# Sliding-window attention and a mixer layer on one core: the first channel weight loaded as full rows in two tiles, batch 1's scores in 64-row bursts without padding, and batch 0's output product by thirds of its weight

## The chip, the cores and the metric

The kernel runs on one core of a Trainium2 chip. The metric is the device time of one execution in microseconds (us). The engines are named as the profile names them: PE is the matrix engine (TensorE), DVE the vector engine, ACT the scalar engine, POOL the gpsimd engine and SP the queue that issues most transfers.

## What is computed

Eight batches, eight heads, 576 positions, 64 values per head. Heads 0 to 3 look back over 32 positions, heads 4 to 7 over 128 in steps of 4; a token-mixing and a channel-mixing layer with four weights follow. Inputs and output are float32.

```python
# attention, per batch b and head h (scale 1/8)
scores = scale * q @ k.T                      # 576 x 576, rel = row - column
mask   = (0 <= rel < 32) if h < 4 else (0 <= rel < 128 and rel % 4 == 0)
x[:, 64*h : 64*h+64] = softmax(where(mask, scores, -1e9)) @ v
# mixer, per batch
u   = x + (relu(x.T @ w_tok1) @ w_tok2).T     # w_tok1 576 x 256, w_tok2 256 x 576
out = u + relu(u @ w_ch1) @ w_ch2             # w_ch1 512 x 1536, w_ch2 1536 x 512
```

## The kernel before

**Stages.** The program is a prologue for batch 0 (its attention and token mixing) and then eight stages, `for b in range(B)` (line 1006). The main line of stage b is `gen_main(b)` (line 747): for each of 12 blocks `mb` of the hidden layer a product `gp` with the first channel weight (line 768), a relu into the tile `gt` (line 771), and then the output product `yp` of `gt` with the second channel weight `w4` (lines 787 and 807), to which `u` is added on the way out (line 797). Batches go in pairs: an odd batch also carries the 64 last positions of both (`gt` at line 759, `yp` at line 807). Beside the main line, stage b holds the attention values and token mixing of batch b+1 and the transposes and scores of batch b+2; stage 0 holds all of batch 1's attention as well, since the prologue covers batch 0 alone.

**Who sets the order.** All order is written by hand. `interleave` (line 816) walks through the main line, which yields the time that its author gave each piece, and drops each step of a list `(due time, cost, function)` in once that clock has passed the due time. Within an engine instructions run in the order in which they were emitted; between engines they wait on semaphores. So a due time sets a place in five queues at once (PE, DVE, ACT, POOL and SP), and every DMA that a step issues takes its place in SP's or POOL's queue.

**Scores.** Two forms exist. `scores_plain` and `scores_dil` (lines 453 and 479) serve batches 0 and 1: one matmul per head and block over 128 rows, in which the other head's 64 rows of queries are zero (the tile `qz`), and ahead of each a matmul with the identity that puts a large negative number (`veil`) where the mask forbids (line 423). `scores_twin` (line 498) serves batches 2 to 7 (`twinned`, line 345): the two heads of a pair stand on rows 0 to 63 and 64 to 127, a matmul for each in turn (line 510), with no padding and no veil; the mask is multiplied in after the exponential by POOL (`mask` and `mask_tails`, lines 552 and 567). A burst `g` covers two head pairs in six PSUM banks and 24 matmuls. `bare_steps` (line 363) makes the transposed queries and keys for batch 2's bursts on PE; from batch 3 on the transposes are DMAs (`dma_steps`), and POOL copies the keys into place (`place_steps`). `values` (line 592) multiplies with v; `mix_steps` (line 729) places token mixing (`h1p`, `up`) and the transposes `tpu` of `u`, whose copies `uT` feed the next stage's `gp`.

**PSUM.** There are eight banks: three with the tag `main`, three with `fl`, two with `sc`. A new tile in a bank waits until every reader of the last one there is done. A twin burst takes both `sc` banks, all three `fl` banks and one `main` bank.

**Weights.** `load_w3` (line 858) loads the first channel weight from POOL in three tiles of 512 of the 1536 columns, each as 512 pieces of 512 values, so that block `mb` needs tile `mb // 4` alone. The tiles are issued at lines 878, 881 and 984. The second channel weight `w4` comes in three thirds (line 988), four blocks `mb` each. `gate` (line 855) is a one-element copy on POOL that makes a batch's loads wait for something: batch 2's loads (lines 994 to 1001) wait for the first third of `w4`. POOL also casts nearly all inputs from float32 to float16 (`cast_steps`, line 274; `casts1`, line 981).

## Time and profile before

| | |
|---|---|
| time, median of 3 runs | 288.79 us (288.76 to 289.51) |
| the profiled execution's own time | 289.66 us |
| its span | 287.8 us |
| PE, busy | 276.8 us (96%) |
| POOL, ACT, DVE, busy | 163.0, 134.0, 132.1 us |
| chain that ended last | 80% PE, 8% DMA, 3% DVE, 3% POOL, 2% issue |
| granted clock of PE | 1.00 throughout (its upper level) |

The profile comes from one execution. Its span runs from the first instruction to the last; its own time also holds what lies around that. A matmul's record ends when its result is written, which is later than the moment at which the next can start: matmuls of 128x512 are recorded with 380 ns each and start 217 ns apart (0.65 us for three steps in the timeline of PE). So PE's pauses are read from starts and from the idle time in brackets, and not from its busy share. The first product of batch 0, `gp`, starts at 28.47 us, that of batch 1 at 69.24 us, and that of batch 2 at 105.06 us; these bound the two stages which the change touches. The page's line on DMA shows nine tenths or more in nearly every slice of 7.2 us up to 108 us, with one slice of three tenths (64.8 to 72 us).

### The profile page before, as it was taken

How to read it: one execution, taken by the hardware profiler on the slowest of the kernel's cores; microseconds unless marked ns; L12 is line 12 of the kernel's file. 1: busy time of each engine (PE TensorE's matmuls, PEld its weight loads, DVE VectorE, ACT ScalarE, POOL GpSimd, SP SyncE). 2: the span in 40 equal slices, each digit the busy share in tenths (PEclk: the TensorE clock that was granted, in tenths of full speed). 3: DMA queues.
4: the chain of work that ended last, by engine and by line, in shares of the span. 5: the costliest groups of instructions: out<-in, count | busy, mean ns of one | idle time of the engine just before them, and what ended most of it. 6: DMA issues, size and time to landing. Idle time of an engine off the chain costs nothing.

```text
span 287.8 us, 6995 instructions
## 1 busy us (share of the span) xinstructions
PE 276.8 (96%) x2838; PEld 210.9 (73%) x2838; DVE 132.1 (46%) x278; ACT 134.0 (47%) x265; POOL 163.0 (57%) x221
## 2 busy tenths in 40 slices
PE   5879999999999999999999999999999999999995
PEld 2777676888766886698776976797766966886594
DVE  7747658446764236414640164416440274421022
ACT  2854673263543804574447615482546534225500
POOL 6961860478865799449970999279952930000000
PEclk9999999999999999999999999999999999999999
DMA  7999999993999998979888978299974210431023
GB/s 218 263 211 218 283 225 207 320 218 82 328 210 192 264 264 230 139 164 350 226 159 182 330 224 186 57 219 329 193 150 95 85 64 2 91 112 37 0 76 108
DMA packets 105551, 52.63 MB, mean 183 GB/s; under 512 B 73872, under 2 KB 104464, under 8 KB 105520
## 3 DMA queue, kind: packets, MB, share of 16 engines
q1 hardware_dynamic: 101280, 47.07, 67.0%
q0 software_dynamic: 2640, 3.94, 8.0%
q10 hardware_dynamic: 1600, 1.18, 1.4%
q8 instruction: 22, 0.36, 0.6%
q14 instruction: 9, 0.07, 0.1%
HBM read 37.07 MB, written 9.44 MB: 162 GB/s over the span
## 4 chain that ended last, share of the span: by engine, by line
PE 80%; DMA 8%; DVE 3%; POOL 3%; issue 2%; ACT 2%; ACTq 1%; SPq 0%; POOLq 0%; DVEq 0%
PE yp L787 29%; PE gp L768 24%; DMA l_vd<-in_v_dram 4%; PE h1p L627 4%; PE yp L807 3%; DMA l_k<-in_k_dram 3%; PE up L639 3%; PE sc L510 3%; PE gt L759 3%; DVE xn L112 1%; DMA kr<-c_k 1%; PE h1p L625 1%; PE av L608 1%; PE up L650 1%; PE av L603 1%
## 5 line engine op out<-in xcount | busy, mean ns | idle before, releaser
L787 PE MATMUL yp<-w,gt 128*128 128x256 f16 x756 | 87.1, 273 | 0.0
L787 PEld LDWEIGHTS <-gt 128*128 128x128 f16 x768 | 78.6, 106 | 6.5
L106 ACT ACTIVATE gt<-gp 128x512 f16<-128x512 f32 x69 | 41.2, 597 | 76.3 <-PE gp L768 76.0
L768 PE MATMUL gp<-utd,w 128*128 128x512 f16 x144 | 54.7, 380 | 0.0
L768 PE MATMUL gp<-utm,w 128*128 128x512 f16 x144 | 54.6, 379 | 0.0
L768 PEld LDWEIGHTS <-w 128*128 128x128 f16 x384 | 39.2, 114 | 20.3 <-issue 0.5
L797 DVE TENSOR_TENSOR o<-yp,u 128x512 f32<-128x512 f32 x31 | 21.4, 691 | 63.1 <-PE yp L787 58.5
L112 POOL TENSOR_TENSOR attp<-attp,const 128x1280 f16<-128x1280 f16 x12 | 31.4, 2616 | 27.5 <-ACT attp L534 27.4
L112 DVE TENSOR_TENSOR xn<-av,rec 128x320 f16<-128x320 f32 x64 | 31.4, 491 | 2.2
L112 POOL TENSOR_TENSOR attd<-attd,const 128x1024 f16<-128x1024 f16 x12 | 25.3, 2132 | 1.6 <-ACT attd L534 1.6
L768 PE MATMUL gp<-uT,w 128*128 128x512 f16 x96 | 25.8, 379 | 0.0
L108 DVE TENSOR_SCALAR gt<-gp 128x512 f16<-128x512 f32 x27 | 18.5, 686 | 13.6 <-PE gp L768 13.1
L645 DVE TENSOR_TENSOR u<-up,xn 128x512 f16<-128x512 f32 x26 | 17.9, 690 | 7.5 <-PE up L639 7.5
L534 ACT ACTIVATE attp<-sc 128x480 f16<-128x480 f32 (+1 forms) x36 | 16.1, 536 | 7.4 <-PE sc L510 7.4
L102 POOL CAST c_k<-l_k 128x512 f16<-128x512 f32 x29 | 18.0, 628 | 1.9 <-DMA l_k<-in_k_dram 1.7
L102 POOL CAST c_q<-l_q 128x512 f16<-128x512 f32 x27 | 16.8, 629 | 3.1 <-DMA l_q<-in_q_dram 3.1
L616 DVE RECIPROCAL rec<-av 128x5 f32<-128x5 f32 x64 | 12.2, 190 | 13.8 <-PE av L613 13.7
L106 ACT ACTIVATE h<-h1p 128x256 f16<-128x256 f32 x29 | 11.1, 384 | 14.5 <-PE h1p L627 14.1
L399 POOL COPY kt<-kr 128x512 f16<-128x512 f16 x10 | 10.7, 1075 | 9.0 <-DMA kr<-c_k 9.0
L697 ACT COPY utd<-utm 128x512 f16<-128x512 f16 x12 | 12.8, 1135 | 4.1 <-DMA utm<-u 4.1
L102 POOL CAST vv<-l_vn 128x256 f16<-128x256 f32 x32 | 12.0, 420 | 4.3 <-DMA l_vn<-in_v_dram 4.1
L112 POOL TENSOR_TENSOR attt<-attt,const 128x512 f16<-128x512 f16 x12 | 14.0, 1165 | 0.0
(147 smaller groups left out, 459.9 us busy)
## 6 DMA issues: line engine op xcount, KB each, us to landing
out_dram<-o SPq DMA_DIRECT2D x72, 128.0 KB, 3.1
l_q<-in_q_dram SPq DMA_DIRECT2D x15, 512.0 KB, 7.2
l_k<-in_k_dram SPq DMA_DIRECT2D x14, 512.0 KB, 7.1
l_vn<-in_v_dram SPq DMA_DIRECT2D x32, 128.0 KB, 6.6
l_vd<-in_v_dram SPq DMA_DIRECT2D x16, 256.0 KB, 4.6
w<-in_moe_w_ch_dram POOLq DMA_DIRECT2D x6, 512.0 KB, 7.6
lt<-in_q_dram SPq DMA_DIRECT2D x8, 128.0 KB, 4.6
l_vt<-in_v_dram SPq DMA_DIRECT2D x8, 128.0 KB, 4.9
```

The source lines that it names most:

```text
L102: eng.tensor_copy(out=out, in_=in_)
L106: nc.scalar.activation(out=out, in_=in_, func=AF.Relu)
L108: eng.tensor_scalar_max(out=out, in0=in_, scalar1=0.0)
L112: eng.tensor_tensor(out=out, in0=x, in1=y, op=ALU.mult)
L534: nc.scalar.activation(out=out, in_=in_, func=AF.Exp, scale=0.125)
L616: nc.vector.reciprocal(out=rec[:, :, 0], in_=av[:, :, 64])
L627: nc.tensor.matmul(out=p, lhsT=w[:, s, j], rhs=x[:, s, c], start=False, stop=(s == 3))
L645: nc.vector.tensor_tensor(out=u16(b, s), in0=blocks4(p), in1=blocks4(xn[b][:, s]), op=ALU.add)
L697: nc.scalar.copy(out=natural(uTd[:, cb - 2]), in_=uTm[i][:, cb].rearrange("p r m -> p m r"))
L768: nc.tensor.matmul(out=p, lhsT=w3_block(cb, mb), rhs=uT[(b, cb)][0], start=(i == 0), stop=(i == 3))
L787: nc.tensor.matmul(out=p[:, c], lhsT=gta[:, mb, a0:m0 + 512:4] if half else gta[:, mb, a0:a0 + 128], rhs=w4[mb][:, c], start=(mb == 0), st ...
L797: nc.vector.tensor_tensor(out=blocks4(o32), in0=blocks4(p), in1=u16(b, s), op=ALU.add)
```

## The change

- `load_w3` loads 256 of the 512 rows at a time, each row of 1536 values whole, into two tiles. Every block `mb` now needs both. Both are issued in the prologue: the first behind the first of batch 0's two `vd` casts and no longer ahead of both, the second in its old place. The third load is gone.
- Batch 1 becomes twinned. Its transposes come from `bare_steps(1)`. In its first burst the mask is multiplied in by POOL after the exponential, pair by pair; in its second the six banks are first filled with the veil by 20 matmuls with the identity (128 columns each), over which the score matmuls add.
- Batch 0's output product runs for row groups 0 to 2 side by side in the three `main` banks, a third of `w4` at a time; row group 3 follows as before.
- The relu of batch 0's blocks 0 to 7, 9 and 11 is on DVE (before: the odd ones).
- Two query casts and the two `vd` casts of batch 1 move from POOL to ACT; `w4`'s loads stand after the same cast as before, with two casts fewer ahead of them. Batch 2's gate and loads move behind batch 1's first mask on POOL.
- Due times in stages 0 and 1 are new. Among them: batch 2's first burst stands between the last transposes of batch 1's `u` and the first product of stage 1, and batch 3's two bursts come later among the output products of stage 1.

```diff
-    w3 = [fixed(f"w3_{i}", [128, 4, 512]) for i in range(3)]
+    w3 = [fixed(f"w3_{i}", [128, 2, DCH]) for i in range(2)]
...
     def twinned(b):
-        return b >= 2
+        return b >= 1
...
-        if b == 2:
+        if b <= 2:
             tags = tags[2:4] + tags[0:2] + tags[4:6]
...
+        veils = b == 1 and g == 1
+
         def twin(hp, banks, c, keys, queries):
+            ends = c.stop == (512 if banks is not small else 256)
             for h in range(2):
                 rows = slice(64 * h, 64 * h + 64)
-                n = c.stop - c.start
-                nc.tensor.matmul(out=banks[h][:, c], lhsT=keys(rows), rhs=queries(rows), start=True, stop=True)
+                nc.tensor.matmul(out=banks[h][:, c], lhsT=keys(rows), rhs=queries(rows),
+                                 start=not veils, stop=ends or not veils)
+
+        if veils:
+            for p in ps:
+                for r in range(4 if p not in small else 2):
+                    nc.tensor.matmul(
+                        out=p[:, 128 * r:128 * r + 128], lhsT=ident,
+                        rhs=veil[:, BLK + 128:BLK + 256] if p in small else veil[:, 0:128],
+                        start=(r == 0), stop=False)
...
-                if h and (g or b == 2):
+                if h and b == 1 and hp == 0:
+                    mask(0)
+                    mask_tails(0)
+                elif h and (b == 2 or (g and b > 2)):
...
+        if b == 1 and g == 0:
+            mask(1)
+            mask_tails(1)
...
-            return w3[mb // 4][:, cb, mb % 4:512:4]
+            c0 = 512 * (mb // 4)
+            return w3[cb // 2][:, cb % 2, c0 + mb % 4:c0 + 512:4]
...
-            relu(nc.vector if (mb % 2 == 1 if b == 0 else mb % 4 != 3 if b == 1 else mb in (1, 5)) else nc.scalar, gta[:, mb, m0:m0 + 512], p)
+            relu(nc.vector if (mb < 8 or mb % 2 == 1 if b == 0 else mb % 4 != 3 if b == 1 else mb in (1, 5)) else nc.scalar, gta[:, mb, m0:m0 + 512], p)
...
+        if b == 0:
+            ps3 = [bank("main", 3, f"yp_{b}_{s}") for s in range(3)]
+            for i in range(3):
+                for s, p in enumerate(ps3):
+                    for half in range(2):
+                        c = slice(256 * half, 256 * half + 256)
+                        for mb in range(4 * i, 4 * i + 4):
+                            nc.tensor.matmul(
+                                out=p[:, c],
+                                lhsT=gta[:, mb, s:512:4] if half else gta[:, mb, 128 * s:128 * s + 128],
+                                rhs=w4[mb][:, c], start=(mb == 0 and not half), stop=(mb == NMB - 1 and bool(half)))
...
-        c = slice(512 * i, 512 * i + 512)
-        nc.gpsimd.dma_start(out=w3[i], in_=moe_w_ch1[:, c].rearrange("(x p) c -> p x c", p=128))
+        nc.gpsimd.dma_start(
+            out=w3[i], in_=moe_w_ch1[256 * i:256 * i + 256, :].rearrange("(x p) c -> p x c", p=128))
...
-    load_w3(0)
     cast_vd(0, 0, nc.gpsimd)
+    load_w3(0)
     cast_vd(0, 2, nc.gpsimd)
     load_w3(1)
...
-    load_w3(2)
-    for i in (2, 3, 4, 5, 7, 6, 8, 9, 10, 11):
+    for i in (0, 1, 2, 3, 4, 6, 8, 9, 10, 11):
         casts1[i]()
...
+            steps += [(t, 0.25, f) for t, f in zip((2.8, 3.4, 5.0, 5.4, 6.0, 9.6, 10.2, 10.8, 11.4), bare)]
+            steps += score_steps(1, 7.2, 5.6, lag=0.25)
+            steps += [(6.2 + 0.6 * i, 0.0, lambda i=i: cast_qk(1, "q", 2 + i, nc.scalar)) for i in range(2)]
+            steps += at(9.0, 0.0, [loads2])
+            steps += [(12.5 + 0.1 * i, 0.0, lambda i=i: cast_vd(1, 2 * i, nc.scalar)) for i in range(2)]
...
-            scores2 = score_steps(2, 29.6, 4.4, lag=0.25)
+            scores2 = score_steps(2, 34.2, 4.4, lag=0.25)
...
-            steps += score_steps(3, 21.0, 4.6, lag=0.1)
+            steps += score_steps(3, 25.4, 4.6, lag=0.1)
```

How instructions stand at three places. First POOL in the prologue; `w` with 4x512 or 2x1536 is the first channel weight, `vv` and `vt` the casts of batch 0's v, `lt` the gate ahead of batch 1's loads. Before:

```order
L860 DMA w_0_84<-in_moe_w_ch_dram 128x4x512
L102 CAST vv_69<-l_vd_123 128x4x2x64 x2
L860 DMA w_1_85<-in_moe_w_ch_dram 128x4x512
L102 CAST vt_71<-l_vx_124 128x4x64
L883 DMA w1t_80<-in_moe_w_tok_dram 64x256
L885 COPY w2p_82<-w_81 128x512
L885 COPY w2p_83<-w_81 128x512
L856 CAST lt_589<-w2p_83 1x1
L102 CAST c_t_609<-lt_589 128x512
L102 CAST c_q_611<-l_q_0_585 128x512
L860 DMA w_2_86<-in_moe_w_ch_dram 128x4x512
```

After:

```order
L102 CAST vv_69<-l_vd_122 128x4x2x64
L904 DMA w_0_84<-in_moe_w_ch_dram 128x2x1536
L102 CAST vv_69<-l_vd_122 128x4x2x64
L904 DMA w_1_85<-in_moe_w_ch_dram 128x2x1536
L102 CAST vt_71<-l_vx_123 128x4x64
L928 DMA w1t_80<-in_moe_w_tok_dram 64x256
L930 COPY w2p_82<-w_81 128x512
L930 COPY w2p_83<-w_81 128x512
L901 CAST lt_588<-w2p_83 1x1
L102 CAST c_t_608<-lt_588 128x512
```

The first load moved behind one `vd` cast, the second kept its place, and the third, which stood among batch 1's casts, is gone. Second, DVE at the end of stage 0: `o` is the output of batch 0, `kt` and `kr` are batch 2's keys, `uT` the transposed `u` of batch 1, `gt` the first relu of stage 1. Before:

```order
L102 COPY uT_0_1240<-tpu_0_1239 128x640
L102 COPY uT_3_1254<-tpu_3_1253 128x640
L797 TENSOR_TENSOR o_0_2_1215<-yp_2_1214,u_0_499 128x512
L102 COPY uT_1_1282<-tpu_1_1281 128x640
L387 COPY kr<-tp_k_2_1303 128x512
L388 COPY kt<-tp_k_2_1303 128x128
L387 COPY kr<-tp_k_3_1316 128x512
L388 COPY kt<-tp_k_3_1316 128x128
L797 TENSOR_TENSOR o_0_3_1296<-yp_3_1295,u_0_499 128x512
L108 TENSOR_SCALAR gt<-gp_0_1346 128x512
```

After:

```order
L842 TENSOR_TENSOR o_0_3_1102<-yp_3_1101,u_0_498 128x512
L385 COPY kt<-tp_k_0_1187 128x512
L102 COPY uT_0_1208<-tpu_0_1207 128x640
L385 COPY kt<-tp_k_1_1215 128x512
L102 COPY uT_3_1222<-tpu_3_1221 128x640
L102 COPY uT_1_1230<-tpu_1_1229 128x640
L108 TENSOR_SCALAR gt<-gp_0_1291 128x512
```

The last output, two key copies and all three `uT` copies now stand in one row, with the relu of stage 1 right behind. Third, PE in stage 1, where batch 3's first burst `sc_3_0` begins. Before, among the 64 last positions' output product `yp_1_4`:

```order
L807 LDWEIGHTS gt_93
L807 MATMUL yp_1_4_1703<-w4_87,gt_93 128x512
L510 LDWEIGHTS kt_65
L510 MATMUL sc_3_0_0_1716<-qt_66,kt_65 128x160
L510 LDWEIGHTS kt_65
L510 MATMUL sc_3_0_1_1717<-qt_66,kt_65 128x160
```

After, among the next output product `yp_1_0`:

```order
L832 LDWEIGHTS gt_92
L832 MATMUL yp_1_0_1691<-w4_86,gt_92 128x256
L512 LDWEIGHTS kt_65
L512 MATMUL sc_3_0_0_1718<-qt_66,kt_65 128x160
L512 LDWEIGHTS kt_65
L512 MATMUL sc_3_0_1_1719<-qt_66,kt_65 128x160
```

The burst moved behind all of `yp_1_4` and three quarters of `yp_1_0`; the second burst moved from ahead of `yp_1_1` into `yp_1_2`.

## Rows read from the trace of the kernel before

**Rows 1.** Windows, by stage: elapsed us, then each engine's busy us; granted clock, DMA share, GB/s

```profile
28.47:69.24 40.77, 40.11 (x462) 31.88 (x460) 24.67 (x54) 20.26 (x42) 24.43 (x42) 1.00 0.99 233
69.24:105.06 35.82, 35.22 (x376) 26.22 (x375) 17.59 (x35) 17.34 (x36) 26.81 (x27) 1.00 0.98 243
105.06:287.80 182.74, 179.00 (x1728) 135.70 (x1726) 70.88 (x146) 81.41 (x155) 94.45 (x114) 1.00 0.64 153
```

**Rows 2.** Timeline, PE: start, us, line, tiles, shape; spacing of batch 1's score matmuls

```profile
36.03 0.19 PE L425 MATMUL sm<-qz,kt 128*128 128x64 f16 x1
...
36.18 0.19 PE L423 MATMUL sm<-veil,const 128*128 128x64 f16 x1
...
39.12 0.22 PE L425 MATMUL sc<-qz,kt 128*128 128x128 f16 x1
...
39.29 0.22 PE L423 MATMUL sc<-veil,const 128*128 128x128 f16 x1
```

**Rows 3.** Line 423's matmuls, batches 0 and 1 together: counts by shape

```profile
L423 PE MATMUL sc<-veil,const x56: 216/219/233, 7.9 to 42.3; 128*128 128x128 f16 x32, 128*128 128x160 f16 x24
L423 PE MATMUL sm<-veil,const x40: 190/193/220, 11.7 to 43.1; 128*128 128x64 f16 x32, 128*128 128x128 f16 x8
```

**Rows 4.** Chain of waits, 60 to 72 us: batch 2's two score bursts; start, us

```profile
60.51 0.75 PE sc L510 x24
...
70.26 0.71 PE sc L510 x24
```

**Rows 5.** Timeline, PE: the pauses of both stages, idle time and releaser in brackets

```profile
40.65 0.19 PE L423 MATMUL sm<-veil,const 128*128 128x64 f16 x1 [0.20 <-ACT attd L488]
...
48.70 0.30 PE L608 MATMUL av<-vv,attd 128*128 128x65 f16 x4 [0.20 <-DVE xn L112]
...
82.35 0.28 PE L625 MATMUL h1p<-xn,w1t 128*128 128x256 f16 x1 [0.39 <-DVE xn L112]
...
91.53 0.44 PE L510 MATMUL sc<-qt,kt 64*128 64x160 f16 x8 [0.21 <-POOL kt L399]
```

**Rows 6.** Timeline, POOL and PE, and line 860's landing times: the first channel weight

```profile
19.65 0.74 POOL L860 DMA_DIRECT2D w<-in_moe_w_ch_dram  x1
...
28.47 0.99 PE L768 MATMUL gp<-uT,w 128*128 128x512 f16 x3
...
DMA to landing us min/median/max: 6.9/7.8/7.8
```

**Rows 7.** Timeline, DVE: copies out of PSUM at the end of batch 0's stage

```profile
59.89 0.69 DVE L385 COPY kt<-tp_k 128x512 f16<-128x512 f16 x1 [0.35 <-PE tp_k L378]
...
64.06 0.49 DVE L102 COPY uT<-tpu 128x640 f16<-128x640 f16 x1 [1.29 <-PE tpu L667]
64.99 0.82 DVE L102 COPY uT<-tpu 128x640 f16<-128x640 f16 x1 [0.44 <-PE tpu L675]
65.73 0.68 DVE L797 TENSOR_TENSOR o<-yp,u 128x512 f32<-128x512 f32 x1
```

**Rows 8.** Timeline, ACT: batch 2's exponentials and a copy among them

```profile
62.46 1.53 ACT L534 ACTIVATE attp<-sc 128x480 f16<-128x480 f32 x3
63.81 0.76 ACT L100 COPY uT<-tpu 128x640 f16<-128x640 f16 x1
```

**Rows 9.** Timeline, PE and POOL: batch 4's first burst, its last mask, its first masked use

```profile
122.38 0.64 PE L510 MATMUL sc<-qt,kt 64*128 64x160 f16 x14
...
136.68 1.16 POOL L112 TENSOR_TENSOR attt<-attt,const 128x512 f16<-128x512 f16 x1
...
138.32 0.28 PE L608 MATMUL av<-vv,attd 128*128 128x65 f16 x4
```

**Rows 10.** Timeline, POOL, and line 988's issues and landing times: the second channel weight

```profile
42.81 0.41 POOL L102 CAST vt<-l_vx 128x256 f16<-128x256 f32 x1
...
L988 POOL DMA_DIRECT2D w<-in_moe_w_ch_dram x3: 541/548/548, 39.2 to 40.3; - x3
...
DMA to landing us min/median/max: 5.5/7.4/10.6
```

More of the change, by code (lines that the diff above doesn't have):

```diff
@@ L990, with loads2 @@
             in_=moe_w_ch2[512 * i:512 * i + 512, :].rearrange("(p i) c -> p i c", i=4))
-    for cast in casts1[12:]:
-        cast()
-    new_qk(2)
-    gate(l32[(2, "t")][0:1, 0, 0:1], w4[0][0:1, 0:1])
-    for nm in ("q", "k"):
-        load_tail(2, nm, nc.sync)
-    for h0 in (0, 4):
-        for nm in ("q", "k"):
-            load_qk(2, nm, h0, h0 + 4, nc.sync)
-    load_v(2)
+    casts1[12]()
+    casts1[13]()
+    cast_vx(1, nc.gpsimd)
+    def loads2():
+        new_qk(2)
+        gate(l32[(2, "t")][0:1, 0, 0:1], w4[0][0:1, 0:1])
+        for nm in ("q", "k"):
+            load_tail(2, nm, nc.sync)
+        for h0 in (0, 4):
+            for nm in ("q", "k"):
+                load_qk(2, nm, h0, h0 + 4, nc.sync)
+        load_v(2)
     def at(t0, dt, fs):
```

55 lines of the change are left out of this document (34 added, 21 removed).

## The prediction

> **What bounds the kernel.** I read the windows first. From 28.47 to 105.06 us, the stages of batches 0 and 1, PE is busy for 40.11 of 40.77 and 35.22 of 35.82 us at a granted clock of 1.00 (its upper level, 2.4 GHz); the reader is to see that PE bounds both, with 0.66 + 0.60 = 1.26 us of recorded idle time, while no other engine is busy for more than 32 us of 40 [rows 1]. After 105.06 the order of the work is unchanged; whatever is won must be won before. Two quantities decide: PE's column time, and its pauses. Since a 512-column record lasts 0.38 us but the next one starts 0.217 us later, a pause hides up to 0.16 us more than its bracket shows.
>
> **What is removed.** Batch 1's padded scores. The spacing of their matmuls is 0.15 us for five steps of 64 columns (0.03 each) and 0.17 us for three of 128 (0.057), so about 0.07 for 160 [rows 2]. Line 423 has, for batches 0 and 1 together, 24 matmuls of 160 columns, 32 + 8 of 128 and 32 of 64 [rows 3]; batch 1 has half, and line 425 one score matmul for each: 24 x 0.07 + 40 x 0.057 + 32 x 0.03 = 4.9 us. In their place stand two twin bursts, of 0.75 and 0.71 us as batch 2's are [rows 4], and 20 veil matmuls of 128 columns, 20 x 0.057 = 1.14: 2.6 us. **Gain 2.3 us**, all on PE and so on the path. The transposes of batch 1's queries and keys are as many columns as before, and the thirds of `yp` are the same 72 matmuls in another order: no change.
>
> The pauses of the two stages go too, since what they wait for moves. The four largest are 0.20 (exponentials of batch 1), 0.20 and 0.39 (`xn` on DVE) and 0.21 us (`kt` on POOL) in brackets [rows 5]; with 0.16 hidden in each, and the remaining 0.26 of recorded idle time, I get 1.9 to 2.4. **Gain 2.2 us**, near the upper end, since the small ones hide time as well. This is the generous half of the sum: it takes all that was there, and what comes is listed by itself.
>
> **What is added: six places where PE may wait.**
> - *First weight.* Block 0 of batch 0 now needs both tiles, the second at its third matmul: 28.47 + 0.43 = 28.9 us. The old second tile was issued at 19.65 us and landed 6.9 us later, at 26.6, and the old third had not been issued [rows 6]. Half a megabyte more now travels by then. If the larger pieces cost nothing extra the tile lands near 27; with the 3.5 us more that a tile's worth takes (landing at 23.1 after 7.8, then at 26.6), near 30.1. So 0 to 1.2; I take 0.25, nearer the early end, as a row of 1536 values goes in fewer, longer pieces.
> - *Bursts of batch 1.* The first waits for DVE's copy of the last-but-one key transpose: 0 to 0.2, taken 0.2 (a copy lasts 0.69, the steps are placed 0.6 apart).
> - *Keys.* Two transposes of batch 1 share a bank, whose two copies together last about one `kt` copy of 0.69 us [rows 7]: 0 to 0.25, taken 0.25.
> - *The end of stage 0.* The order of DVE shows the last output, `kt`, `uT`, `kt`, `uT`, `uT` in one row: 0.68 + 0.69 + 0.49 + 0.69 + 0.82 + 0.49 = 3.9 us [rows 7]. PE meanwhile has only three transposes of batch 2, four of `u` and batch 2's first burst, 2.6 us by the spacings above, and uses the last `uT` at the third matmul of `gp`, 0.65 (with two spacings and the first one's own) later: 3.9 - 3.25 = 0.6 us at the least. But one bank of the burst is that of `tpu_3`, free only after the fifth copy, 3.4 us into the row, where PE arrives after 2.0: 1.4 us. And one `tpu` must wait for ACT's `uT` copy of 0.76 us, which has stood behind exponentials of 0.51 us each [rows 8]: 2.0 us. I take 1.4.
> - *Batch 2's last key transpose* waits for a copy of queries on ACT, behind all exponentials of that batch: 0 to 0.6 (one exponential of 0.51 [rows 8] and the rest of a second), taken 0.4.
> - *Batch 3's masks.* In batch 4, from the start of a first burst to the end of the last mask it took 136.68 + 1.16 - 122.38 = 15.5 us, and the use followed at 138.32, with 0.5 to spare [rows 9]. By the order of the change PE reaches the same use 14.1 to 14.7 us after the first burst (three and a quarter output products of 2.6, two bursts, four `gp` of 0.87, small ones). Pause 0 to 0.8, taken 0.4, as that is the middle and POOL is idle at its start.
>
> Together 0.25 + 0.2 + 0.25 + 1.4 + 0.4 + 0.4 = **2.9 us come**, between 0.6 and 5.05.
>
> A rule of the Trainium skill speaks to the fourth place: "TensorEngine Tiling (Array Packing)", section Performance Considerations, says that tiling raises TensorE's throughput but not the rate at which PSUM is emptied. This trace agrees: a burst of 24 takes PE 0.75 us [rows 4], three of its exponentials alone 1.53 [rows 8]. By that rule alone the fourth term would be its upper end and the saving 1.0 us.
>
> **What costs nothing, and its cover.** The third load leaves POOL, and no engine waits for that place. Four more relus on DVE (0.69 us or less each) fall on stretches of four `gp` matmuls (0.87 us); if DVE's `xn` steps fall behind them, PE's pauses of the old kind come back. POOL gets four masks for batch 1 (of about 1.2 us [rows 9], the wide ones more) and loses four casts; it was busy for 24.43 us of 40.77 [rows 1], idle for longest right after the gate of batch 2, which is where the masks fall. ACT takes over four casts and was busy for half the stage [rows 1]. Batch 1's loads land about 1 us later, as the longer weight tiles are ahead of them, and the transposes that need them are placed some 0.5 to 1 us behind that; if that is gone, the first weight's wait simply moves there. The second weight is issued about 1 us sooner, since two casts ahead of it went; its first use is after 44 us, when before it had landed at 44.7.
>
> **The sum.** -2.3 - 2.2 + 2.9 = -1.6 us. The profiled execution has a span of 287.8 us and a time of 289.66, which is 0.87 above the median of 288.79; its span becomes 286.2, its time 288.06, and the same saving on the median gives **287.2 us**. With the ends: -2.3 - 2.4 + 0.6 = -4.1 (284.7) and -2.3 - 1.9 + 5.05 = +0.85 (289.6).
>
> **The rivals.**
> 1. *The banks turn over in time* (chance 0.24). The copies on DVE start before the last output does, and the DMA lands early: only 1.0 us of pauses come, and -2.3 - 2.2 + 1.0 = -3.5 gives 285.3. For it: DVE is busy for 24.67 of 40.77 us [rows 1], so no queue is long. Against it: the six copies have one row in the order.
> 2. *The waits eat the gain* (0.20). The places come at their upper ends, 4.5 to 5: 288.7 to 289.3, no change that can be told. For it: DMA is at 0.98 to 0.99 in both stages [rows 1], so a late load is late by much. Against it: six ends at once.
> 3. *Batch 1's v comes too late: slower* (0.14). The `vd` casts now stand on ACT, ahead of the second burst's exponentials, due near 44.6 us; before they stood on POOL, and the last cast of v ran at 42.81 [rows 10]. The second weight is now issued 1 us sooner beside v's loads; its last third took 10.6 us to land where others flew beside it, its first 5.5 [rows 10]. If `vd` lands that same 5.1 us later, near 48, ACT stands still, `sc` banks stay full and PE waits 3.3 us: -1.6 + 3.3 = +1.7, 290.5. It decides only from a landing later than about 45. Against it: v's loads are issued ahead of the weight's. The skill's "DMA: Bandwidth & Descriptors", section Queues, rings and completion order, has each DMA engine go round between queues packet by packet; the 10.6 against 5.5 us agrees, and by that a load issued earlier can still be overtaken.
>
> **How the numbers follow.** A measurement can tell 0.3%, 0.87 us, from no change. My forecast has 0.42, with its own range 286.2 to 288.3, a sixth of which lies within 0.87 us of before. Faster by more: 0.24 + 0.36 = 0.60. Within: 0.06 + 0.17 = 0.23. Slower: 0.14 + 0.03 (the second rival's tail) = 0.17. The range from 284.7 to 289.7 takes in the bounds and leaves out the third rival and a little of the first.
>
> **What would show it right or wrong.** In the changed profile PE's bursts of batch 1 should last about 0.75 and 0.71 us with 1.1 of veil, and `gp` of batch 2 start near 103.5 instead of 105.06, with 182.7 us from there to the end. The pauses should stand before batch 2's first burst or `gp_1_0` (61 to 68 us, released by DVE), at batch 2's last key transpose (ACT), and at batch 3's first masked values near 102 us (POOL). A third matmul of `gp_0_0` released by DMA much after 28.9 would show the first term mis-sized. The forecast is wrong if new pauses exceed 4.5 us, if `vd` holds ACT at 45 us, or if batch 2's stage no longer starts and runs as before.

## The result, and the profile after

The changed kernel takes 289.71 us (median of 20 runs), the kernel before 288.77 in the same runs: the ratio is 1.0043, with a 95% interval from 1.0023 to 1.0063. It is slower by 0.94 us, where 287.2 was forecast and 289.7 was the end of the range. Its runs also spread more, from 288.4 to 292.2 us, against 287.7 to 289.6 before. Medians here and below are of all runs, while the ratios leave out four slow ones, two of them at a granted clock of 0.75 throughout (360.42 us in experiment 6 and 358.82 us in experiment 8, where it is the profiled one, so that no row of experiment 8's profile is used).

The profile after comes from an execution of 289.61 us, at the median. The page's part 1 first, then the windows by stage (elapsed us, busy us of each engine, granted clock, DMA share, GB/s), cut at the first products of batches 0 to 3:

```profile
PE 275.1 (96%) x2810; PEld 208.4 (72%) x2810; DVE 131.3 (46%) x276; ACT 134.3 (47%) x267; POOL 166.6 (58%) x220
```

```profile
26.71:67.54 40.83, 37.08 (x418) 28.35 (x415) 23.64 (x49) 16.39 (x34) 23.48 (x38) 1.00 0.98 248
67.54:104.14 36.60, 36.26 (x396) 27.19 (x391) 17.94 (x38) 21.47 (x46) 27.16 (x27) 1.00 0.89 200
104.14:133.58 29.44, 28.87 (x293) 22.01 (x292) 12.72 (x27) 15.11 (x30) 24.43 (x30) 1.00 1.01 238
133.58:287.83 154.25, 150.30 (x1438) 113.69 (x1436) 58.11 (x119) 66.29 (x125) 73.63 (x87) 0.99 0.59 143
```

These answer to [rows 1]. Stage 0 is as long as before (40.83 against 40.77 us), but PE is busy for 37.08 of it instead of 40.11. Its work did shrink; the time was waited away. About 0.9 of these 3.03 us was only moved: sixteen transposes of batch 2, which stood in stage 0, now stand in stage 1, and that stage is longer by them. Stage 2 is longer by one pause, the last of those below. The page's chain of waits has 75% PE and 13% DMA, where it had 80% and 8%.

The pauses stand in the timeline of PE after (idle time and releaser in brackets):

```profile
28.55 2.78 PE L787 MATMUL gp<-uT,w 128*128 128x512 f16 x12 [1.25 <-DMA w<-in_moe_w_ch_dram]
...
32.34 0.40 PE L378 MATMUL tp_q<-const,c_q 128*128 128x128 f16 x4 [0.34 <-POOL c_q L102]
...
45.34 1.92 PE L811 MATMUL yp<-w,gt 128*128 128x256 f16 x16 [0.57 <-DMA w<-in_moe_w_ch_dram]
...
64.46 0.38 PE L682 MATMUL tpu<-const,u 128*128 128x128 f16 x4 [0.56 <-ACT uT L100]
...
66.08 0.23 PE L512 MATMUL sc<-qt,kt 64*128 64x160 f16 x1 [0.16 <-DVE kt L385]
66.81 0.63 PE L512 MATMUL sc<-qt,kt 64*128 64x160 f16 x13 [0.50 <-DVE uT L102]
...
71.30 0.38 PE L378 MATMUL tp_k<-const,c_k 128*128 128x128 f16 x4 [0.31 <-ACT qt L383]
...
109.55 0.20 PE L629 MATMUL av<-vt,attt 128*128 128x65 f16 x1 [0.57 <-POOL attt L112]
```

The reader is to see three kinds: waits for DMA or for a cast of what it brought (28.55, 32.34, 45.34), waits for copies out of shared banks (64.46 to 71.30), and one for a mask (109.55). With the 0.16 us that each bracket hides they are those of the table further below.

### The profile page after: what moved, and what is told of

The parts are those of the page before. It is cut to its first block, busy times and chain, and to the rows that moved or that the text cites. A ratio compares the mean times of both kernels' runs of the same rounds, so it can differ in the third digit from the quotient of the medians.

```text
span 287.8 us, 6938 instructions
## 1 busy us (share of the span) xinstructions
PE 275.1 (96%) x2810; PEld 208.4 (72%) x2810; DVE 131.3 (46%) x276; ACT 134.3 (47%) x267; POOL 166.6 (58%) x220
## 4 chain that ended last, share of the span: by engine, by line
PE 75%; DMA 13%; POOL 3%; DVE 2%; ACT 2%; issue 2%; SPq 1%; ACTq 1%; POOLq 0%
PE gp L787 23%; PE yp L832 23%; DMA l_k<-in_k_dram 6%; PE h1p L645 5%; PE up L657 4%; PE gt L778 4%; PE yp L852 4%; PE yp L811 3%; PE sc L512 2%; DMA w<-in_moe_w_ch_dram 2%; DMA l_vx<-in_v_dram 2%; DMA utm<-u 2%; PE h1p L643 1%; PE av L626 1%; PE av L621 1%
## 5 line engine op out<-in xcount | busy, mean ns | idle before, releaser
L832 PE MATMUL yp<-w,gt 128*128 128x256 f16 x684 | 77.9, 273 | 0.0
L832 PEld LDWEIGHTS <-gt 128*128 128x128 f16 x696 | 71.4, 106 | 5.6
L106 ACT ACTIVATE gt<-gp 128x512 f16<-128x512 f32 x65 | 38.9, 598 | 65.4 <-PE gp L787 65.1
L112 POOL TENSOR_TENSOR attp<-attp,const 128x1280 f16<-128x1280 f16 x14 | 36.6, 2612 | 35.1 <-ACT attp L545 35.0
L842 DVE TENSOR_TENSOR o<-yp,u 128x512 f32<-128x512 f32 x28 | 19.4, 691 | 59.8 <-PE yp L832 55.3
L108 DVE TENSOR_SCALAR gt<-gp 128x512 f16<-128x512 f32 x31 | 21.2, 686 | 16.3 <-PE gp L787 15.6
L787 PE MATMUL gp<-uT,w 128*128 128x512 f16 x96 | 24.4, 380 | 1.2 <-DMA w<-in_moe_w_ch_dram 1.2
L545 ACT ACTIVATE attp<-sc 128x480 f16<-128x480 f32 (+1 forms) x42 | 18.7, 540 | 14.7 <-PE sc L512 14.7
L112 POOL TENSOR_TENSOR attt<-attt,const 128x512 f16<-128x512 f16 (+1 forms) x14 | 15.2, 1089 | 0.0
L545 ACT ACTIVATE attd<-sc 128x512 f16<-128x512 f32 x28 | 14.4, 612 | 0.0
```

The costliest lines, as they stand in the source:

```text
L106: nc.scalar.activation(out=out, in_=in_, func=AF.Relu)
L108: eng.tensor_scalar_max(out=out, in0=in_, scalar1=0.0)
L112: eng.tensor_tensor(out=out, in0=x, in1=y, op=ALU.mult)
L545: nc.scalar.activation(out=out, in_=in_, func=AF.Exp, scale=0.125)
L787: nc.tensor.matmul(out=p, lhsT=w3_block(cb, mb), rhs=uT[(b, cb)][0], start=(i == 0), stop=(i == 3))
L832: nc.tensor.matmul(out=p[:, c], lhsT=gta[:, mb, a0:m0 + 512:4] if half else gta[:, mb, a0:a0 + 128], rhs=w4[mb][:, c], start=(mb == 0), st ...
```

## Experiments

The first theory (A) was that the first weight as whole rows holds up stage 0; its rivals were the end of stage 0 (B) and the late masks of batch 3 (C).

**1. The first weight in columns again**, in the changed kernel:

```diff
-    w3 = [fixed(f"w3_{i}", [128, 2, DCH]) for i in range(2)]
+    w3 = [fixed(f"w3_{i}", [128, 4, 512]) for i in range(3)]
...
-            return w3[cb // 2][:, cb % 2, c0 + mb % 4:c0 + 512:4]
+            return w3[mb // 4][:, cb, mb % 4:512:4]
...
+        c = slice(512 * i, 512 * i + 512)
+        nc.gpsimd.dma_start(out=w3[i], in_=moe_w_ch1[:, c].rearrange("(x p) c -> p x c", p=128))
...
+    load_w3(2)
```

> The changed kernel with the first weight in three tiles of 512 columns again (third load among batch 1's casts); the order of the prologue stays as changed. If the whole-row tiles are what costs (A), the wait of 1.25 us at the third matmul of the first product goes, batch 1's loads land some 1 to 1.5 us sooner and the two waits of 0.5 and 0.3 us at batch 1's first transposes go with it: 1.5 to 2 us less than the changed kernel, about 288.0. If the loss sits at the end of stage 0 (B) or in the late masks (C), it stays within 0.5 us of the changed kernel, 289.2 to 290.2.

Measured: 289.43 us, ratio 1.0037 (1.0020 to 1.0055): no different from the change. The wait at the first product and those at the first transposes went, but PE then reached the ninth block before the third tile and waited 1.3 us there (1.14 in brackets):

```profile
38.00 0.41 PE L786 MATMUL gp<-uT,w 128*128 128x512 f16 x1 [1.14 <-DMA w<-in_moe_w_ch_dram]
```

So in this kernel it is not the form of the load: either form makes PE wait.

**2. The new order of the prologue in the kernel before:**

```diff
-    load_w3(0)
     cast_vd(0, 0, nc.gpsimd)
+    load_w3(0)
```

> The kernel before with one edit: the first weight tile is issued behind the first of batch 0's two vd casts instead of ahead of both. In the changed kernel's trace the first product of batch 0 starts at 26.7 instead of 28.5 us, and I put that down to this order (v's loads no longer share the DMA engines with the weight, vt is cast 1.7 us sooner). If that is right, the first product starts near 26.8 here too and, as the first weight in columns needs one tile alone, up to 1.5 us come through: 287.3 to 288.3. If the earlier start has another cause, or the DMA sets the pace of stage 0 anyway, 288.5 to 289.0.

Measured: 288.85 us, 1.0013 (0.9995 to 1.0031): no gain. The first product started at 26.6 us, but stage 0 then lasted 42.55 us; PE waited 0.98 us in brackets for the cast of batch 1's first queries:

```profile
31.08 0.29 PE L309 MATMUL tp_q<-const,c_q 128*128 128x128 f16 x2 [0.98 <-POOL c_q L102]
```

These queries landed at 30.27 us, no earlier than in the first profile of the kernel before (30.06). Nor was the start at 26.6 us a lead: the unedited kernel, profiled again (experiment 12), starts its first product at 26.89 us, and there the queries land at 28.46.

**3 and 4. The burst behind the product; the masks earlier:**

```diff
-            steps += scores2[:10]
...
+            steps += [(0.8 + 0.25 * i, c, f) for i, (_, c, f) in enumerate(scores2[:10])]
```

> The changed kernel with batch 2's first burst moved from ahead of the first product of stage 1 to behind its first two matmuls. B: the 1.0 us before and in the burst (0.32 and 0.68 us) go, and at most 0.3 comes back where the third matmul of the product waits for the last uT; about 0.7 us less, 289.0. A or C: no change within 0.3 us, 289.4 to 290.0, since then another wait takes the place (ACT's exponentials and the values of batch 2 behind them).

```diff
-            steps += score_steps(3, 25.4, 4.6, lag=0.1)
+            steps += score_steps(3, 23.4, 4.6, lag=0.1)
```

> The changed kernel with both bursts of batch 3 due 2.0 earlier in stage 1 (23.4 instead of 25.4). C: the pause of 0.73 us at 108.8 us (the values of head 4 of batch 3 wait for POOL's last mask) goes, 0.6 to 0.8 us less, about 289.0. Against C: the keys' copies or the output bank of the earlier place stop PE for as long, 289.4 to 290.0.

Measured: 293.62 us (1.0178, 1.0153 to 1.0203) and 290.77 (1.0059, 1.0031 to 1.0087). Both missed. With the burst later, PE waited for ACT at batch 2's last transposes, and in stage 2 it stood still for batch 4's keys (the timeline of PE of that kernel):

```profile
70.15 0.38 PE L378 MATMUL tp_q<-const,c_q 128*128 128x128 f16 x4 [0.83 <-ACT attt L545]
71.26 0.33 PE L378 MATMUL tp_k<-const,c_k 128*128 128x128 f16 x3 [0.73 <-ACT qt L383]
...
125.35 0.38 PE L512 MATMUL sc<-qt,kt 64*128 64x160 f16 x6 [1.64 <-POOL kt L399]
126.68 0.44 PE L512 MATMUL sc<-qt,kt 64*128 64x160 f16 x8 [0.94 <-POOL kt L399]
```

POOL copies those keys from a DMA that SP issued at 119.39 us instead of 115.22 and that landed at 124.10 instead of 118.49.

With the masks earlier, the pause at batch 3's values went and two came inside the burst itself, 0.30 and 0.41 us: an exchange. The second, as the timeline of PE has it:

```profile
92.88 0.23 PE L512 MATMUL sc<-qt,kt 64*128 64x128 f16 x2 [0.23 <-DVE u L663]
```

The profile has DVE's `u` end it; POOL's copies of these keys had been done since 90.74 us.

**5 and 6. Fewer bytes, the same matmuls.** This tells DMA from PE. In both kernels the second half of the first weight (rows 256 to 511) is left out and the first half used twice:

```diff
-            return w3[cb // 2][:, cb % 2, c0 + mb % 4:c0 + 512:4]
+            return w3[0][:, cb % 2, c0 + mb % 4:c0 + 512:4]
...
-    load_w3(1)
```

> The changed kernel without the second tile of the first weight: blocks 2 and 3 of the contraction use the first tile again (the second half of the first channel weight is left out). No matmul less, 0.75 MB less of DMA ahead of batch 1's loads. If stage 0 is paced by what the DMA engines bring (first weight, batch 1, second weight, one behind the other), the wait of 1.25 us at the first product and those of 0.5, 0.3 and 0.7 us behind it all shrink: 2 to 3 us less than the changed kernel, 286.7 to 287.7. If PE's own pauses at the end of stage 0 are what costs, the first wait alone goes and is partly found again later: 288.5 to 289.3.

```diff
-            return w3[mb // 4][:, cb, mb % 4:512:4]
+            return w3[mb // 4][:, cb % 2, mb % 4:512:4]
...
-in_=moe_w_ch1[:, c]
+in_=moe_w_ch1[0:256, c]
```

> The kernel before with the same bytes left out (each of its three tiles loaded for the first 256 rows only, blocks 2 and 3 use blocks 0 and 1; the second half of the first channel weight is left out). If DMA paces stage 0 in both kernels, this one gains too, but less, since its PE has 2.3 us more to do in that stage: 287.6 to 288.3, and the changed kernel without these bytes is the faster of the two by 0.5 to 1.5 us. If not, no change: 288.3 to 288.8.

Measured: the changed kernel without these bytes 287.29 us (0.9960 of before, 0.9945 to 0.9975), which is 2.4 less than with them; the kernel before without them 288.04 (0.9986, 0.9971 to 1.0001), hardly less. Stage 0 in the windows of the first, then of the second:

```profile
26.82:64.99 38.17, 36.70 (x418) 28.65 (x415) 23.60 (x49) 16.29 (x34) 23.63 (x38) 1.00 0.98 244
```

```profile
26.69:67.45 40.76, 40.11 (x461) 31.87 (x459) 24.66 (x54) 20.26 (x42) 25.13 (x41) 1.00 0.94 226
```

In the kernel before PE needs 40.8 us for the stage with these bytes or without. In the changed kernel PE could be done in 38.2 and DMA does not let it. One load shows it, the first of batch 1's queries, issued at 22.5 to 22.8 us (KB, us to landing): in the kernel before (experiment 12), in the changed kernel, and in the changed kernel without these bytes:

```profile
l_q<-in_q_dram SPq DMA_DIRECT2D x1, 512.0 KB, 5.6
```

```profile
l_q<-in_q_dram SPq DMA_DIRECT2D x1, 512.0 KB, 8.8
```

```profile
l_q<-in_q_dram SPq DMA_DIRECT2D x1, 512.0 KB, 5.9
```

This is the larger part of the miss: DMA stood close behind PE. Of the 2.4 us, 1.8 stand in the profiles, where stage 0 takes 39.99 us in the mean of the changed kernel's four (experiments 13 to 15 and the one above); these four executions average 289.20 us, 0.5 below the median.

**7. The burst ahead of the transposes of `u`**, as in the kernel before:

```diff
-            scores2 = score_steps(2, 34.2, 4.4, lag=0.25)
+            scores2 = score_steps(2, 29.6, 4.4, lag=0.25)
```

(and batch 2's five transposes at their old due times)

> The changed kernel with batch 2's first transposes and first burst back where they stood before (among the output products of batch 0, ahead of the transposes of u). If the row of DVE copies and the shared banks at the end of stage 0 cost (B), the pauses of 0.72, 0.32 and 0.68 us there go and little comes: 1.0 to 1.7 us less, 288.0 to 288.7. If batch 2's loads set the time of that burst (its last key tile lands at 58.7 us), PE waits for them instead and the time stays at 289.2 to 290.

Measured: 291.20 us, 1.0094 (1.0061 to 1.0127). PE did not wait for batch 2's loads, as the rival had it, but for the banks that the burst had filled: a `tpu` stood for 1.38 us in brackets until ACT had done the exponentials:

```profile
66.98 0.38 PE L691 MATMUL tpu<-const,u 128*128 128x128 f16 x4 [1.38 <-ACT attt L545]
```

**8 to 11. Three places edited, alone and together.** The second weight issued earlier, batch 2's transposes earlier, batch 3's keys cast on DVE and its steps earlier:

```diff
-    for i in (0, 1, 2, 3, 4, 6, 8, 9, 10, 11):
+    for i in (0, 1, 2, 3, 4):
         casts1[i]()
...
-    casts1[12]()
-    casts1[13]()
+    for i in (6, 8, 9, 10, 11, 12, 13):
+        casts1[i]()
...
-zip((28.0, 30.0, 30.5, 31.4, 32.2), bare)
+zip((25.5, 26.3, 27.2, 28.2, 29.2), bare)
...
-            casts = cast_steps(3)
+            casts = cast_steps(3, nc.vector)
...
```

> The changed kernel with the second weight's loads issued two key casts and four v casts earlier on POOL (behind batch 1's fourth query or key cast, before the wait for l_k's second half). In the changed kernel the DMA engines are only half busy near 36 and 40 us, POOL waits for that l_k until 36.2, and PE waits 0.73 us for the first third of the weight. If what is lost is this lull and not DMA work as such, the third lands before 44.4, the pause goes, and batch 2's loads behind the gate come earlier by as much: 0.5 to 0.9 us less, 288.8 to 289.2. If the weight only takes v's place on the engines, v comes late for the values of batch 1 and nothing is won: 289.5 to 290.

> The changed kernel with batch 2's first five transposes 2.5 to 3.2 us earlier, between the output products and the u products of stage 0; the burst stays. The two key copies of 0.68 us then no longer stand between the last output and the last uT copies on DVE. If that row makes the pauses at the end of stage 0 (0.72, 0.32 and 0.68 us), about 1 to 1.4 us go: 288.3 to 288.8. If DMA paces this place too (batch 2's keys are cast at 55.8 to 57.5 us), the transposes wait and it stays at 289.4 to 290.

> The changed kernel with batch 3's key casts moved from POOL (behind batch 2's masks) to DVE, its query casts, DMA transposes, key copies and both bursts 2 us earlier. The edit before moved the bursts alone and only exchanged the pause of 0.73 us at the masks for 0.72 us at POOL's key copies. If those copies were late because POOL did batch 2's masks first, both pauses go: 0.6 to 0.8 us less, 288.9 to 289.1. If not, or if DVE's relus and u come late in turn: 289.5 to 290.2.

> The three edits together (second weight's loads earlier, batch 2's transposes earlier, batch 3's keys on DVE and its bursts earlier). If the pauses are independent places on PE's path, the gains add up: 2.1 to 3.1 us less than the changed kernel, 286.6 to 287.6, below both kernels. If DMA paces the stages, what one place wins is waited for at the next: no better than 288.7.

Measured: 293.44 us (1.0157, 1.0130 to 1.0184), 290.72 (1.0066, 1.0044 to 1.0088), 293.50 (1.0161, 1.0119 to 1.0203) and 298.35 (1.0345, 1.0323 to 1.0367). None won.

The earlier second weight overtook batch 1's v. The lines on DMA (KB each, median us to landing) show v's loads issued from 34.7 to 37.7 us, first in the changed kernel, then with all three edits (where the weight is issued at 35.0 instead of 38.3):

```profile
l_vd<-in_v_dram SPq DMA_DIRECT2D x2, 256.0 KB, 3.6
l_vt<-in_v_dram SPq DMA_DIRECT2D x1, 128.0 KB, 4.2
l_vx<-in_v_dram SPq DMA_DIRECT2D x1, 128.0 KB, 4.3
```

```profile
l_vd<-in_v_dram SPq DMA_DIRECT2D x2, 256.0 KB, 11.9
...
l_vt<-in_v_dram SPq DMA_DIRECT2D x1, 128.0 KB, 12.5
l_vx<-in_v_dram SPq DMA_DIRECT2D x1, 128.0 KB, 11.5
```

And why, from the lines on queues (packets, MB, share of the engines' time) of the latter between 40 and 44 us; q0 carries POOL's loads, q1 those of SP:

```profile
q0 software_dynamic: 204, 0.77, 94.8%
q1 hardware_dynamic: 203, 0.05, 9.6%
```

The two queues move about as many packets, 204 and 203. But 187 of the weight's are 4096 bytes long (the other 17 have 4 bytes), and v's are 256 bytes: so v gets 0.05 of 0.82 MB. ACT and PE show what follows (timelines of both):

```profile
47.96 1.28 ACT L100 CAST vv<-l_vd 128x512 f16<-128x512 f32 x2 [5.18 <-DMA l_vd<-in_v_dram]
```

```profile
49.56 1.01 PE L811 MATMUL yp<-w,gt 128*128 128x256 f16 x4 [2.83 <-ACT attt L545]
```

This is the third rival's chain, link by link, and its price: 2.83 us and what the bracket hides, where 3.3 was worked out. The eighth edit alone came 3.3 us above the changed kernel by the ratios.

The tenth edit's wait was of its own making: the casts of batch 3's keys stand on DVE ahead of `xn` of batch 2, and PE stood still for 2.39 us in brackets (timelines of DVE, POOL and PE):

```profile
76.12 1.75 DVE L102 CAST c_t<-lt 128x512 f16<-128x512 f32 x1
...
79.61 1.65 DVE L102 CAST c_k<-l_k 128x512 f16<-128x512 f32 x1
...
81.80 1.49 DVE L102 CAST c_k<-l_k 128x512 f16<-128x512 f32 x3
```

```profile
75.47 2.12 POOL L112 TENSOR_TENSOR attd<-attd,const 128x1024 f16<-128x1024 f16 x1
...
78.85 2.12 POOL L112 TENSOR_TENSOR attd<-attd,const 128x1024 f16<-128x1024 f16 x1
```

```profile
81.94 0.28 PE L643 MATMUL h1p<-xn,w1t 128*128 128x256 f16 x1 [2.39 <-DVE xn L112]
```

The loads had landed by 75.57 us. Two of the casts lasted 1.75 and 1.65 us, the next three 0.42 to 0.62 us each; the two long ones ran while POOL multiplied wide masks. That this made them long was not tested. The edit also kept the two pauses of 0.30 and 0.41 us in batch 3's first burst, so these were not, as its expectation had it, waits for POOL's copies behind the key casts.

The ninth edit shortened the pauses at the end of stage 0 in its profile (0.29, 0.51 and 0.68 us instead of 0.72, 0.24, 0.32 and 0.68), but put pauses of 0.24, 0.38 and 0.18 us among the `u` products and transposes before them, at 57.6 to 60.5 us: 2.28 us in all instead of 1.97. So it won nothing there. Its median was 1.0 us above the changed kernel's; what makes the rest of that is left open.

**12 to 15. More profiles.** One execution is a thin basis, so both kernels were profiled again, unedited.

> The kernel before once more, unedited, for a second profile: the profiled execution shown with it took 289.66 us, 0.9 above its median, and is no fair partner for the changed kernel's. In a profile near the median the first product of batch 0 should start before 28.5 us or stage 0 should be shorter than 40.8 us, and the product of batch 3 start near 132.8 instead of 133.8 us.

> The changed kernel once more, unedited, for a second profile. Its runs spread from 288.4 to 292.2 us, those of the kernel before from 287.6 to 289.6. In the profile at hand v's last loads of batch 1 land at 39.0 to 41.4 us, 3 to 4 us before they are needed, and the second weight is issued at 38.3. If the long runs are those in which the second weight overtakes v (as in the edit that issued it earlier, where v landed at 48 to 50 us), a run near 291 or above shows v's last loads landing after 45 us and a wait at the values or the output product of stage 0; one near 289 shows them before 43. If the length comes from the first weight, the wait at the first product is longer instead.

> As the run before: the changed kernel unedited. Long (290.5 and above) with v's last loads after 45 us, or short with them before 43, if the second weight overtaking v makes the spread.

> As the two runs before: the changed kernel unedited. Long (290.5 and above) with v's last loads after 45 us, or short with them before 43, if the second weight overtaking v makes the spread.

Measured: 288.01 us for the kernel before, 288.81, 288.86 and 289.51 for the changed one. The starts of the first products (timelines of PE) give the length of each stage:

```
                       first product   stage 0   stage 1   stage 2   from there to the end
before                        28.47     40.77     35.82     28.70    154.06
before, again                 26.89     40.85     35.70     28.70    154.04
changed                       26.71     40.83     36.60     29.44    154.25
changed, again (r2)           27.38     39.34     36.60     29.44    154.26
changed, again (r3)           27.05     39.73     36.60     29.44    154.26
changed, again (r4)           27.38     40.06     36.60     29.43    154.26
```

So the late first product of the first profile (28.47) was that execution's own, and not what the change improved. Stages 1 and 2 repeat to 0.1 us; stage 0 of the changed kernel varies by 1.5 us, with the wait for the first weight (0.2 to 1.4 us) and the one for the second (0 to 0.7). No execution of 290.5 us or more was caught, so whether the long runs are those in which v is overtaken stays open.

**16 to 18. The pauses behind the weights taken off.** Batch 1's third `u` transpose copied by ACT, batch 2's last queries by DVE, batch 2's transposes earlier, batch 3's last mask on DVE:

```diff
-        eng = nc.scalar if cb == 2 else nc.vector
+        eng = nc.scalar if cb == 2 or (b == 1 and cb == 3) else nc.vector
...
+            if nm == "q" and b == 2 and hp >= 2:
+                nc.vector.tensor_copy(out=qta[:, hp], in_=grid)
...
-            mult(nc.gpsimd, t, t, tails_seen[g])
+            mult(nc.vector if b == 3 and g else nc.gpsimd, t, t, tails_seen[g])
```

> The changed kernel with batch 2's first transposes earlier (as in the edit tried alone), and three pieces of work on another engine: batch 1's third u transpose copied by ACT instead of DVE, batch 2's last two query copies by DVE instead of ACT, batch 3's last mask by DVE instead of POOL. The pauses aimed at are those behind the DMA's: 1.96 us at the end of stage 0, 0.47 at batch 2's last key transpose, 0.73 at batch 3's values. If what PE wins behind the second weight is not taken back by DMA, 2 to 3 us less than the changed kernel: 286.7 to 287.8, below both kernels; in a profile the product of batch 3 starts near 131 us instead of 133.6. If the loads of batches 2 and 3 pace these places as well: 289 to 290.

Measured: 289.27 us, 1.0051 (1.0023 to 1.0080). Of the pauses aimed at, the one at batch 2's last key transpose shrank to 0.14 us and the one at batch 3's values went (stage 2 took 28.72 us); at the end of stage 0, with those among the `u` products, 1.60 us were left of 1.97. But the mask on DVE waited for ACT with the output sum queued behind it, and the next product had no bank until 104.6 us:

```profile
102.99 0.94 DVE L112 TENSOR_TENSOR attt<-attt,const 128x512 f16<-128x512 f16 x1 [4.55 <-ACT attt L547]
103.85 0.68 DVE L844 TENSOR_TENSOR o<-yp,u 128x512 f32<-128x512 f32 x1
```

The last two put that mask ahead of the two wide ones on POOL instead, with the first weight in columns (third tile one cast earlier) and in rows:

```diff
-                elif h and (b == 2 or (g and b > 2)):
+                elif h and (b == 2 or (g and b > 3)):
...
+            elif b == 3:
+                mask(2)
+                mask(3)
```

> The changed kernel with the first weight in three tiles of columns, the third issued behind the first cast of batch 1 (one cast earlier than before), batch 2's first transposes earlier, batch 1's third u transpose copied by ACT, batch 2's last two query copies by DVE, and batch 3's last tail mask ahead of its two wide masks on POOL (instead of DVE, where it held up the output sum behind it for 1.0 us). Neither the first nor the last blocks of stage 0 wait for the weight as long, and the pauses behind are off: stage 0 about 37.8, stage 1 36.1, stage 2 28.7 us against 40.85, 35.7 and 28.7 in the kernel before: 286.0 to 287.2, faster than both. If DMA takes it back (a later second weight, v overtaken): 288.3 and above.

> As the run beside it, but with the first weight in whole rows as in the changed kernel. The mask's new place removes the 1.0 us that the edit before brought; the waits for both row tiles (0 to 1.6 us) and for batch 1's first loads stay: 287.4 to 288.4, that is 0.8 to 1.8 us behind the kernel with columns if the form of the first weight costs, the same if only the sum of bytes counts.

Measured: in columns 288.70 us, 0.9999 of before (0.9976 to 1.0021); in rows 289.45, 1.0024 (0.9994 to 1.0054). What these edits took off behind the weights brings the change, in columns, back to where it started, and not ahead. The two differ by 0.75 us, just under what was expected if the form of the first weight costs, but their intervals overlap: whether the form costs in this version is left open. The windows of the one in columns:

```profile
26.75:67.14 40.39, 37.61 (x418) 28.33 (x415) 22.93 (x48) 17.32 (x35) 24.37 (x39) 1.00 1.05 251
67.14:103.52 36.38, 36.35 (x395) 27.22 (x391) 18.53 (x40) 20.51 (x44) 27.10 (x27) 1.00 0.91 209
103.52:132.27 28.75, 28.75 (x292) 21.93 (x291) 12.74 (x27) 15.10 (x30) 24.49 (x30) 1.00 1.01 234
```

Stage 0 lasts 40.39 us with PE busy for 37.61. The wait for the third tile is still there, though the tile was issued one cast earlier (at 29.84 us, to land at 38.36), and so are 0.57 and 0.26 us at batch 1's first query transposes:

```profile
38.40 0.41 PE L791 MATMUL gp<-uT,w 128*128 128x512 f16 x1 [1.29 <-DMA w<-in_moe_w_ch_dram]
```

No version that beats the kernel before was found.

## Why the prediction was wrong

**What is removed: right.** In the timeline of PE the first burst of batch 1 takes 0.91 us, 0.16 of it a wait, the second 0.67, and the veil 1.21: 2.63 where 2.6 was worked out from [rows 2, 4]. The 96 matmuls in whose place they stand take 4.82 us at their usual spacings, where 4.9 was worked out: a gain of 2.2 us, where 2.3 was taken. The pauses of the kernel before [rows 5] did go. Counted as starts beyond the usual spacing (those of 0.13 us or more), in its second profile, these were 2.85 us, where 2.2 was taken.

**What is added: the step that failed.** The term of the sum was 2.9 us, with 5.05 as its upper end. In the four profiles of the changed kernel, counted the same way, the places gave:

```
place                              taken   measured (mean of four)
both tiles of the first weight      0.25   0.95   (0.2 to 1.4)
batch 1's first query transposes    0      0.86   (waits for casts of loads)
first third of the second weight    0      0.26   (0 to 0.73)
bursts and keys of batch 1          0.45   0.47
end of stage 0                      1.4    1.97
batch 2's last key transpose        0.4    0.47
batch 3's masks                     0.4    0.73
a value product in stage 1          0      0.19
sum                                 2.9    5.9
```

-2.2 - 2.85 + 5.9 = +0.85 us. Stages 0 to 2 of the same profiles are 0.78 us longer than in the kernel before (106.03 against 105.25), and 0.2 us more at the very end of the span was not looked into; the medians say 0.94. Of the 3.0 us by which this term was short, the first three lines make 0.70 + 0.86 + 0.26 = 1.82, all of it DMA. Two steps failed there. One is the sentence under "What costs nothing": that batch 1's loads land about 1 us later behind a margin of 0.5 to 1 us, and that the second weight lands before its use. The first of batch 1's queries landed 1.6 us behind the first product in both profiles of the kernel before, and 3.7 to 4.8 us behind it in the four of the changed kernel: 2.1 to 3.2 us later, and not 1. The prediction had the price at hand, 3.5 us for a tile's worth, half a megabyte, and used it for the tile but not for the loads behind it. The second weight was issued at 38.3 to 39.1 us, no sooner than in the second profile of the kernel before (38.1), and its first third landed at 44.0 to 45.3, when PE was ready for it at 44.2 to 45.2. The other is the size of the first weight's term, 0.25: the second tile took 10.1 to 11.2 us to land, where 6.9 was known and 10.4 allowed for at most. The warning stood in [rows 1]: a DMA share of 0.99 through stage 0. I took it for a rival's support and not for a second bound. Experiments 5 and 6 show it for one: 2.4 us against 0.3.

Not all of it is DMA: the other 1.2 us of the shortfall are the end of stage 0, the masks and three small places. And two of the prediction's own signs of being wrong came true: new pauses above 4.5 us, and a stage of batch 2 that no longer runs as before (29.44 us instead of 28.70).

**The end of stage 0** was mis-sized, 1.97 instead of 1.4, and close to the upper end of 2.0. The waits were for ACT's and DVE's copies of transposes (64.46 to 66.81 in the lines above); no exponential was part of it, as batch 2's first one ran at 67.70 us. The Trainium skill's rule there ("TensorEngine Tiling (Array Packing)", Performance Considerations), that tiling does not speed up the emptying of PSUM, would have given that end, but by the exponentials of a burst, which is not how it came about. The trace agrees with the rule in experiment 7, where a `tpu` behind the burst waited 1.38 us for them.

**Batch 3's masks** came near their upper end (0.73 of 0.8), and by the mechanism that was forecast: in the changed kernel the last mask ends 15.4 us after the start of the first burst (94.07 to 109.50), and PE was ready for it after 14.75, where 15.5 and 14.1 to 14.7 were worked out. The "near 102 us" among the signs does not follow from that count; the wait stands at 109.

**The rivals.** The second came true and beyond: the waits ate the gain. Its six places gave 4.59 us, as it had them at 4.5 to 5, with three at or near their upper ends (the first weight, the end of stage 0, the masks); 1.31 us more came from places that the sum had put at nothing, and 0.2 was too little for it. The first did not come true on either count: the copies on DVE started at 63.82 us, behind the last output at 63.21, and the DMA landed late. The third did not happen in the profiles of the change, where `vd` landed at 39.5 to 41.8 us, but it lay only 3 us away: issued at 35.0 instead of 38.3, the second weight overtook v, `vd` was cast at 47.96 and the price was near the one worked out. The 10.6 against 5.5 us by which the prediction sized it show less than it read in them: the three thirds of the second weight are issued within 1.1 us on one queue, and the last waits behind the other two: they land at 44.69, 47.15 and 50.81 us [rows 10]. The Trainium skill's rule ("DMA: Bandwidth & Descriptors", Queues, rings and completion order), that an engine goes round between its queues packet by packet, agrees with experiment 11 by its count, 204 packets to 203, if what the profile counts as a packet is what takes its turn, which no run shows. What it makes of the time depends on the size of the packets, which is read from the trace.

**The profile to start from.** The forecast took its saving from a profile with a first product at 28.47 us. That did no harm to the terms that compare stages. But the first weight's landing was set against a third matmul at 28.9 us, and in the changed kernel PE was ready for it at 27.1 to 27.8. And reading the early start of the changed kernel (26.71) as a gain would have been an error, as the second profile of the kernel before shows (26.89).

## What to carry to other kernels

Where PE and DMA are both near full in a stage, a saving on PE is worth only the distance to DMA: before counting what PE saves, list for each load its landing and its first use, move the first uses earlier by the saving, and move every landing by the bytes that the change puts ahead of it. Leaving bytes out while keeping all matmuls is a cheap way to measure that distance, in both kernels. And the moment at which a load is issued is part of the schedule: issued 3.3 us earlier, the second weight in pieces of 4 KB took 0.77 of 0.82 MB while v, in pieces of 256 bytes, was under way.

## What the hardware showed

A wait can cost more than its length. In the last kernel (rows, experiment 18) PE waited 1.80 us in brackets for the first weight, and the granted clock then fell to its lower level, 1.2 GHz, for some 3 us (the wait, and the windows ahead of, in and behind that stretch):

```profile
28.97 0.55 PE L792 MATMUL gp<-uT,w 128*128 128x512 f16 x1 [1.80 <-DMA w<-in_moe_w_ch_dram]
```

```profile
24.00:26.70 2.70, 2.64 (x30) 2.11 (x28) 2.31 (x7) 0.89 (x3) 0.00 (x0) 1.00 1.09 207
26.70:29.00 2.30, 0.50 (x4) 0.04 (x2) 0.69 (x1) 0.44 (x1) 0.00 (x0) 1.00 1.16 243
29.00:32.30 3.30, 3.30 (x9) 1.18 (x10) 1.30 (x2) 0.00 (x0) 0.79 (x2) 0.52 1.10 308
32.30:36.00 3.70, 3.70 (x30) 2.34 (x29) 2.50 (x6) 1.07 (x2) 2.17 (x4) 0.97 1.16 307
```

Seven products there started 0.43 instead of 0.22 us apart and two more 0.33 and 0.34, 1.7 us more. In experiment 11 the clock fell behind both of its long waits, 2.83 us (49.56) and 2.39 us (86.86):

```profile
49.56:52.50 2.94, 2.94 (x23) 2.15 (x23) 1.03 (x4) 2.18 (x5) 2.94 (x2) 0.50 0.03 8
86.86:90.00 3.14, 3.14 (x15) 1.92 (x16) 1.35 (x3) 0.89 (x2) 3.14 (x6) 0.50 1.51 154
```

In the fourth experiment nearly the same wait as in the last kernel, 1.74 us in brackets, left the clock at 1.00, and in the tenth so did one of 2.39 us. So this falls on some executions and not on others. It is at most a part of why kernels with the first weight in rows have runs of 291 to 293 us where those in columns (experiments 1 and 17) ended at 291.1 and 290.0: of the changed kernel's three longest runs, 291.68, 291.93 and 292.19 us, only the first has a mean granted clock below 1.000 (0.993). What makes the other two long stays open.
